# One PV run per eight units throughout, with one score unit in eight copied out of PSUM by VectorE

## The chip, the cores and the metric

One NeuronCore of a Trainium2 chip runs the whole program. The metric is the device time of one execution in microseconds. The engines are TensorE (PE; its weight loads are shown apart as PEld), VectorE (DVE), ScalarE (ACT), GpSimd (POOL) and SyncE (SP, which issues most DMAs).

## The reference

A gated sum of full attention (32 heads of 16, sequence 2048, width 512) and a SwiGLU block (inner width 1792), in float32:

```python
g = sigmoid((x * gate_w).sum(-1, keepdims=True))
q, k, v = split_heads(x @ wqkv)                    # H = 32, Dh = 16, S = 2048
a = concat_heads(softmax(q @ k.T * Dh ** -0.5) @ v) @ wo
b = (silu(x @ w1) * (x @ w3)) @ w2                 # D = 512, F = 1792
return g * a + (1 - g) * b
```

## The kernel before

A prologue (to 82 us) transposes x, splits it into a high and a low part (products of float32 accuracy are made from three products of such halves), projects v and the first heads' q and k, and bounds the scores. A tail of some 32 us ends the output projection. Between them lies the main phase, of which this case speaks. It has two streams of work that TensorE runs interleaved:

- *Attention*, in 1024 units. A unit is a pair of heads j, a half of the queries, one of 16 key blocks k and a group gq of 512 queries. `score` (L746) makes its scores: two matmuls (one per head, 50 rows each, side by side in the two row halves of the array) into a PSUM tile S of 128x1024, of which there are two (`psum2`), used in turn. ScalarE's exponential (L756) reads S and writes one of eight SBUF tiles p0 to p7 (NP = 8, list `free`). `pv` (L735) takes two units at a time: their p times V, accumulated over the key blocks in the one bank acc (17 columns for each head and query group, four column strips of the array at once). After the last key block `evac` copies acc to SBUF (L721) and stores it.
- *Products* (`feed`, L686): the remaining q/k projections, then gate and up of SwiGLU (L413), then its down projection (L531) and part of the output projection (L617). A call issues up to two matmuls, one in each row half of the array ("lanes"). A block of such matmuls fills a bank f (three banks): the first half of its sum in one lane, the second in the other, with a tiny VectorE write (tick, L713) between them that carries the order. The second half may start six slots after the first has ended, and a bank is taken again nine slots after its last use. VectorE evacuates the banks (L424 in the q/k stage, L436 and L458 in the gate and up stage, L547 and L550 later). For each gate block ScalarE makes an exponential (L441), and VectorE a scalar step (L442), eight reciprocals of 64 columns (L444) and a product (L462); these small steps are handed out one or two per unit. The ScalarE exponential of a gate block is put behind the score ahead of a PV run.

The order is written out as a string: Q is a score unit, F a call of `feed`, P a `pv` of two units. Each engine runs its instructions in the order of the program, and waits for the others only by semaphores. A PV product (P) is eight fp32 matmuls of 512 columns in two passes; a run of P's is a stretch of them without a Q or F between them. In before the string is made of 78 long periods (8 Q, 21 F, one run of 4 P) and 50 short ones (8 Q, 15 F, two runs of 2 P):

```python
one = "QQFFFFFF" + "QFFF" * 5 + "QPPPP"
two = "QFFF" * 5 + "QPPQQPP"
order = one * LONG + "QQFFF" + two * (SHORT - 1) + "QFFF" * 4 + "QPPQPP"
```

Of the kernel before, what the change touches and what calls it, by code (L numbers as in the profile page):

```python
# [11 lines left out]
AF = mybir.ActivationFunctionType  # L12
# [5 lines left out]
P = 128  # L18
S = 2048
D = 512  # L20
F = 1792
# [6 lines left out]
NPAIR = H // 2  # L28
SCALE = DH ** -0.5
# [4 lines left out]
def gated_mix_kernel(ctx: ExitStack, tc: tile.TileContext, x, wqkv, wo, w1, w3, w2, gate_w, out):  # L34
# [18 lines left out]
    nc = tc.nc  # L53
# [15 lines left out]
    QD = [[dram.tile([D, S], F32, name=f"{n}{p}_d") for p in "HL"] for n in "qk"]  # L69
# [16 lines left out]
    def psum2():  # L86
        return psum.tile([P, 2, 512], F32, name="S", bufs=2)

    def bank():
        return psum.tile([P, 512], F32, name="f", bufs=3)  # L90
# [179 lines left out]
    def load_step(s):  # L270
        half, j = divmod(s, NPAIR)
        load_q(j, half, s % 2)
        load_k(j, s % 2)
        load_guard(j, half, s % 2)
# [35 lines left out]
    splits, issued = [], 0  # L310
# [275 lines left out]
    def divide(k, half):  # L586

        yield from reciprocals(k, half)
        for b in (2 * half, 2 * half + 1):
            for _ in range(5):  # L590
                yield
            if half == 0:
                o, r = slot("hx", F32), slot("gw", F32)
            else:
                both = wk.tile([P, 2, 512], F32, name="od")
                o, r = both[:, 0, :], both[:, 1, :]
            fetch_o(k, b, o, r)
            for _ in range(7):
                yield
            nc.gpsimd.tensor_mul(o, o, r)  # L600
            for _ in range(3):
                yield
            nc.sync.dma_start(N_d[P * k:P * k + P, 512 * b:512 * b + 512], o)
            yield
        if (k, half) == (2, 1):
            load_wo(2)
# [68 lines left out]
    def after(ins, earlier):  # L675
        tc.add_manual_dep(ins.ins, earlier.ins.name,
                          mybir.DependencyInfo(mybir.DependencyClass.Sync, mybir.DependencyReason.DATA),
                          reason="the two halves of the array write a bank in turn")

    def pick(lane, rest, gap):  # L680
        if ready[lane] and (ready[lane][0]["since"] + gap <= clock or gap == 0):
            return ready[lane].pop(0)
        used = len(over) - 3
        if lane <= 1 and (used < 0 or over[used] is not None and over[used] + rest <= clock):
            block = next(source, None)
            if block:  # L686
                over.append(None)
                return dict(block=block, ps=bank(), id=len(over) - 1, n=0, turn=None)
        return None

    def feed(rest=REST, gap=GAP):
        did = 0
        for lane in range(2):
            if lanes[lane] is None:
                lanes[lane] = pick(lane, rest, gap)
        for lane in range(2):
            t = lanes[lane]
            if t is None:
                continue
            product, done, length = t["block"]  # L700
            did += 1
            second = t["turn"] is not None
            ins = product(t["ps"], slice(64 * lane, 64 * lane + 64), t["n"], second)
            if second and t["n"] == 0:
                after(ins, t["turn"])
            t["n"] += 1
            if t["n"] == length:
                lanes[lane] = None
                if second:
                    done(t["ps"])  # L710
                    over[t["id"]] = clock
                else:
                    turn = nc.vector.memset(tick[:, 0:1], 0.0)  # L713
                    after(turn, ins)
                    t.update(n=0, turn=turn, since=clock)
                    ready[1 - lane].append(t)
        return did
# [18 lines left out]
    def pv(two):  # L736
        for j, half, k, gq, n, p in two:
            for h in range(2):
                r = 32 * (2 * gq + h)
                nc.tensor.matmul(acc[r:r + DH + 1, :], V[:, k, 2 * j + h, :], p[:, h, :],  # L740
                                 start=k == 0, stop=k == NT - 1)
            free.append(n)
        if k == NT - 1:
            evac(j, half)

    def score(j, half, k, gq):  # L746
        i = (NPAIR * half + j) % 2
        ps = psum2()
        t = 512 * gq
        for h in range(2):  # L750
            r = 64 * h
            nc.tensor.matmul(ps[:, h, :], Kt[i][r:r + 50, P * k:P * k + P],  # L752
                             Qt[i][r:r + 50, t:t + 512], start=True, stop=True)
        n = free.pop(0)
        p = wk.tile([P, 2, 512], F32, name=f"p{n}")
        nc.scalar.activation(p, ps, AF.Exp, scale=SCALE)  # L756
        return j, half, k, gq, n, p


# [1 line left out]


    NP = 8
    LONG, SHORT = 78, 50
    one = "QQFFFFFF" + "QFFF" * 5 + "QPPPP"
    two = "QFFF" * 5 + "QPPQQPP"
    order = one * LONG + "QQFFF" + two * (SHORT - 1) + "QFFF" * 4 + "QPPQPP"
    free = list(range(NP))

    units = iter([(j, half, k, gq) for half in range(2) for j in range(NPAIR) for k in range(NT) for gq in range(2)])  # L770
    pend, clock = [], 0
    for i, c in enumerate(order):
        clock += 1 if c != "P" else 4
        if c == "Q":
            step = issued // 32 + 1
            if issued % 32 == 6 and step < 2 * NPAIR:
                assert 8 * (ND - 1) - qk_left >= 8 * min(step // 4, ND - 1)
                load_step(step)
            pend.append(score(*next(units)))
            issued += 1  # L780
            while splits and splits[0][0] <= issued:
                splits.pop(0)[1]()
            while soon and order[i + 1] == "P":
                soon.pop(0)()
            if issued % 128 == (40 if issued // 128 == 5 else 12) and 1 <= issued // 128 < 8:
                stages.append(divide((issued // 128 - 1) % 4, (issued // 128 - 1) // 4))
            if small or later and hurry:
                for _ in range(3 if hurry else 1 + (len(small) > (6 if len(over) < 8 * len(chunks) - 16 else 0))):
                    if small or later and hurry:
                        (small or later).pop(0)()  # L790
            if loads and (hurry or issued % 2 or len(over) > 8 * len(chunks) - 12):
                loads.pop(0)()
            for stage in stages[:1]:
                if next(stage, stages) is stages:
                    stages.pop(0)
        elif c == "F":
            feed()
        else:
            pv(pend[:2])
            pend = pend[2:]  # L800
    assert not pend and issued == 64 * NPAIR

    assert lanes[0] is None
    for _ in reciprocals(ND - 1, 1):
# [1 line left out]
    k = ND - 1  # L806
# [8 lines left out]
    for t in (NT // 2 - 2, NT // 2 - 1):  # L815
        ps = bank()
# [62 lines left out]
```

## Time and profile before

| | |
|---|---|
| time, median of 3 runs | 1406.22 us (1405.67 to 1407.54) |
| the profiled execution | 1405.92 us, span 1404.1 us |
| TensorE busy | 1397.0 us (99%) |
| ScalarE busy | 1033.6 us (74%) |
| VectorE busy | 483.6 us (34%) |
| GpSimd busy | 319.3 us (23%) |
| granted TensorE clock | full in all slices |

Times in the profile are counted from the start of the span. Matmuls are pipelined, so a busy TensorE is one that always has a matmul in flight; its pace is read from the distances between starts. A row of the timeline gives start, duration, engine, line, operation, tiles, shapes and count, and in brackets how long the engine had been idle and what ended that.

### The profile page before, as it was taken

How to read it: one execution, taken by the hardware profiler on the slowest of the kernel's cores; microseconds unless marked ns; L12 is line 12 of the kernel's file. 1: busy time of each engine (PE TensorE's matmuls, PEld its weight loads, DVE VectorE, ACT ScalarE, POOL GpSimd, SP SyncE). 2: the span in 40 equal slices, each digit the busy share in tenths (PEclk: the TensorE clock that was granted, in tenths of full speed). 3: DMA queues.
4: the chain of work that ended last, by engine and by line, in shares of the span. 5: the costliest groups of instructions: out<-in, count | busy, mean ns of one | idle time of the engine just before them, and what ended most of it. 6: DMA issues, size and time to landing. Idle time of an engine off the chain costs nothing.

```text
span 1404.1 us, 28806 instructions
## 1 busy us (share of the span) xinstructions
PE 1397.0 (99%) x11399; PEld 821.9 (59%) x11399; DVE 483.6 (34%) x1067; ACT 1033.6 (74%) x1153; POOL 319.3 (23%) x356
## 2 busy tenths in 40 slices
PE   9999999999999999999999999999999999999998
PEld 7866556566566566565565565555545555555556
DVE  4511111564555546555454654511110110110113
ACT  4557777777777777777777777788788878877880
POOL 5113433011011101110110117331323332232240
PEclk9999999999999999999999999999999999999999
DMA  7653564343123423223333336443434443354435
GB/s 205 165 123 98 132 141 113 70 116 77 46 56 85 114 54 80 66 67 96 70 77 68 82 78 170 106 96 82 126 84 97 106 108 69 70 128 108 104 120 178
DMA packets 112670, 141.43 MB, mean 101 GB/s; under 512 B 16400, under 2 KB 70672, under 8 KB 109456
## 3 DMA queue, kind: packets, MB, share of 16 engines
q1 hardware_dynamic: 110384, 135.72, 40.1%
q10 hardware_dynamic: 2144, 3.80, 0.8%
q8 instruction: 92, 1.51, 0.5%
q14 instruction: 50, 0.41, 0.1%
HBM read 90.70 MB, written 48.76 MB: 99 GB/s over the span
## 4 chain that ended last, share of the span: by engine, by line
PE 99%; DVE 0%; ACT 0%; issue 0%; ACTq 0%
PE acc L740 33%; PE f L413 27%; PE S L752 20%; PE f L531 11%; PE S L184 2%; PE f L96 1%; PE f L98 1%; PE f L97 1%; PE f L617 1%; PE acc L338 0%; PE S L97 0%; PE S L96 0%; PE S L98 0%; PE f L158 0%; PE S L158 0%; ACT xH L161 0%
## 5 line engine op out<-in xcount | busy, mean ns | idle before, releaser
L756 ACT ACTIVATE p<-S 128x1024 f32<-128x1024 f32 x1024 | 967.8, 1027 | 300.8 <-PE S L752 300.8
L740 PE MATMUL acc<-p,V 128*17 128x512 f32 x4096 | 474.4, 594 | 0.0
L752 PE MATMUL S<-Qt,Kt 50*128 50x512 f32 x2048 | 403.7, 408 | 1.0 <-DVE V L396 0.7
L752 PEld LDWEIGHTS S<-Qt,Kt 50*128 50x128 f32 x2048 | 183.3, 184 | 185.5 <-ACT p L756 84.9
L740 PEld LDWEIGHTS acc<-p,V 128*17 128x17 f32 x4096 | 102.3, 97 | 272.5 <-issue 272.3
L444 DVE RECIPROCAL sg<-sg 128x64 f32<-128x64 f32 x448 | 209.3, 517 | 49.1 <-issue 47.0
L413 PE MATMUL f<-xH,fl 64*128 64x512 f32 x1088 | 217.5, 392 | 0.0
L413 PE MATMUL f<-xL,fh 64*128 64x512 f32 x1088 | 217.4, 390 | 0.0
L413 PE MATMUL f<-xH,fh 64*128 64x512 f32 x1088 | 217.4, 392 | 0.0
L413 PEld LDWEIGHTS f<-xH,fh 64*128 64x128 f32 x1088 | 104.4, 186 | 23.8
L413 PEld LDWEIGHTS f<-xL,fh 64*128 64x128 f32 x1088 | 104.3, 185 | 23.4
L413 PEld LDWEIGHTS f<-xH,fl 64*128 64x128 f32 x1088 | 104.6, 186 | 22.6 <-POOL fl L314 0.3
L713 DVE MEMSET tick<- 1x1 f32 x190 | 11.2, 59 | 274.5 <-PE f L531 156.1
L313 POOL CAST fh<-fr 128x512 fp32r<-128x512 f32 x34 | 21.6, 636 | 355.7 <-DMA fr<-in_B_w_dram 292.2
L436 DVE COPY gs<-f 128x512 f32<-128x512 f32 x56 | 38.7, 691 | 69.7 <-PE f L413 63.4
L531 PE MATMUL f<-xL,fh 64*128 64x512 f32 x208 | 61.8, 390 | 0.0
L531 PE MATMUL f<-xH,fl 64*128 64x512 f32 x208 | 60.8, 390 | 0.0
L531 PE MATMUL f<-xH,fh 64*128 64x512 f32 x208 | 59.8, 390 | 0.0
L531 PE MATMUL f<-xH,raw 64*128 64x512 f32 x192 | 57.3, 390 | 0.0
L442 DVE TENSOR_SCALAR sg<-sg 128x512 f32<-128x512 f32 x56 | 27.7, 494 | 82.9 <-ACT sg L441 77.6
L600 POOL TENSOR_TENSOR hx<-hx,gw 128x512 f32<-128x512 f32 x8 | 10.3, 1287 | 198.7 <-DMA gw<-r_d 188.2
L721 DVE COPY u<-acc 128x512 f32<-128x512 f32 x32 | 22.1, 692 | 94.7 <-PE acc L740 91.5
(216 smaller groups left out, 1277.0 us busy)
## 6 DMA issues: line engine op xcount, KB each, us to landing
Kt<-kH_d SPq DMA_DIRECT2D x128, 128.0 KB
h_d<-sg SPq DMA_DIRECT2D x56, 256.0 KB
sg<-h_d SPq DMA_DIRECT2D x43, 256.0 KB
fr<-in_B_w_dram SPq DMA_DIRECT2D x42, 256.0 KB
Qt<-qH_d SPq DMA_DIRECT2D x128, 64.0 KB
Kt<-kL_d SPq DMA_DIRECT2D x64, 128.0 KB
Qt<-qL_d SPq DMA_DIRECT2D x64, 64.0 KB
b_d<-y SPq DMA_DIRECT2D x16, 256.0 KB
```

The costliest lines, as they stand in the source:

```text
L96: nc.tensor.matmul(ps, sH, mH, start=first, stop=False)
L184: nc.tensor.matmul(ps[:, i, :], w[i][h][:, k, :], xs[b][:, k, :], start=n == k == 0, stop=n == 2 and k == ND - 1)
L313: nc.gpsimd.tensor_copy(hi, src)
L413: return nc.tensor.matmul(ps, w[i == 1][r, k, :], (xL if i == 2 else xH)[b][r, k, :], start=n == 0 and not second, stop=n == 3 * ND - 1 an ...
L436: nc.vector.tensor_copy(gs, ps)
L442: small.append(lambda: nc.vector.tensor_scalar(sg, sg, 1.0, None, op0=OP.add))
L444: small.append(lambda q=q: nc.vector.reciprocal(sg[:, q:q + 64], sg[:, q:q + 64]))
L531: ins = nc.tensor.matmul(ps, hs[t][q][i == 1][r, P * o:P * o + P], (w2L if i == 2 else w2H)[q][r, o, :], start=n == 0 and not second, stop ...
L721: nc.vector.tensor_copy(u, acc)
L740: nc.tensor.matmul(acc[r:r + DH + 1, :], V[:, k, 2 * j + h, :], p[:, h, :], start=k == 0, stop=k == NT - 1)
L752: nc.tensor.matmul(ps[:, h, :], Kt[i][r:r + 50, P * k:P * k + P], Qt[i][r:r + 50, t:t + 512], start=True, stop=True)
L756: nc.scalar.activation(p, ps, AF.Exp, scale=SCALE)
```

## The change

The order is built from two new periods, 128 in all. Each has 8 units and one run of four P; `wide` has 19 F, `tight` 18, and the total of F's stays 2388 (so 84 wide periods come first, then 44 tight ones). In each period the fifth unit is written D: its scores are copied from S to its SBUF tile p by VectorE (L757 of after), and its exponential is formed in place, p to p, at the letter e (L805), which stands behind the sixth unit. The other seven units keep their exponential from PSUM (L756 before, L760 after). The tile p of a D unit is handed to `pv` as before.

```diff
-    def score(j, half, k, gq):
+    def score(j, half, k, gq, wait):
...
         p = wk.tile([P, 2, 512], F32, name=f"p{n}")
-        nc.scalar.activation(p, ps, AF.Exp, scale=SCALE)
+        if wait:
+            nc.vector.tensor_copy(p, ps)
+            raw.append(p)
+        else:
+            nc.scalar.activation(p, ps, AF.Exp, scale=SCALE)
...
-    LONG, SHORT = 78, 50
...
+    PERIODS, PRODUCTS = 128, 2388
+    tight = "QFFQFFFFQFFQFFFDFFFQeFFFFQQPPPP"
+    wide = "QFFQFFFFQFFFQFFDFFFQFFeFFFQQPPPP"
+    n_wide = PRODUCTS - PERIODS * tight.count("F")
+    order = wide * n_wide + tight * (PERIODS - n_wide)
...
-        clock += 1 if c != "P" else 4
-        if c == "Q":
+        clock += {"P": 4, "e": 0}.get(c, 1)
+        if c in "QD":
...
-            pend.append(score(*next(units)))
+            pend.append(score(*next(units), c == "D"))
...
+        elif c == "e":
+            p = raw.pop(0)
+            nc.scalar.activation(p, p, AF.Exp, scale=SCALE)
```

TensorE before, in the stretch of short periods: two PV runs of eight matmul pairs (rows acc<-p,V) with two score units (S<-Qt,Kt, x4) between them:

```order
L752 MATMUL S<-Qt_109,Kt_112 128x512 x2
L740 MATMUL acc<-p_18340,V 17x512 x2
L740 MATMUL acc<-p_18345,V 17x512 x2
L740 MATMUL acc<-p_18358,V 17x512 x2
L740 MATMUL acc<-p_18369,V 17x512 x2
L752 MATMUL S<-Qt_108,Kt_111 128x512 x4
L740 MATMUL acc<-p_18380,V 17x512 x2
L740 MATMUL acc<-p_18398,V 17x512 x2
L740 MATMUL acc<-p_18409,V 17x512 x2
L740 MATMUL acc<-p_18428,V 17x512 x2
L752 MATMUL S<-Qt_108,Kt_111 128x512 x2
```

TensorE in the changed kernel, at the end of one of its tight periods: two score units, then the whole run:

```order
L752 MATMUL S<-Qt_108,Kt_111 128x512 x4
L740 MATMUL acc<-p_18680,V 17x512 x2
L740 MATMUL acc<-p_18689,V 17x512 x2
L740 MATMUL acc<-p_18704,V 17x512 x2
L740 MATMUL acc<-p_18713,V 17x512 x2
L740 MATMUL acc<-p_18725,V 17x512 x2
L740 MATMUL acc<-p_18736,V 17x512 x2
L740 MATMUL acc<-p_18757,V 17x512 x2
L740 MATMUL acc<-p_18762,V 17x512 x2
L752 MATMUL S<-Qt_109,Kt_112 128x512 x2
```

The two scores that stood between the two half runs now stand ahead of one whole run, so a run of all eight units follows at once. ScalarE in the changed kernel, one period in the gate and up stage (p0 to p7 are the SBUF tiles of its units, S the PSUM tile):

```order
L760 ACTIVATE p0_11932<-S_11929 128x1024
L760 ACTIVATE p1_11943<-S_11940 128x1024
L760 ACTIVATE p2_11960<-S_11957 128x1024
L760 ACTIVATE p3_11972<-S_11969 128x1024
L760 ACTIVATE p5_11998<-S_11995 128x1024
L805 ACTIVATE p4_11985<-p4_11985 128x1024
L760 ACTIVATE p6_12026<-S_12023 128x1024
L760 ACTIVATE p7_12033<-S_12030 128x1024
L441 ACTIVATE sg_11981<-gs_11979 128x512
```

The exponential of the fifth unit (p4) has moved behind that of the sixth (p5), and reads p4 itself; before, ScalarE formed all eight from S in the order of the units. VectorE, another period of the same stage in the changed kernel, around one of the new copies (L757):

```order
L442 TENSOR_SCALAR sg<-sg 128x512
L444 RECIPROCAL sg<-sg 128x64 x5
L713 MEMSET tick 1x1
L444 RECIPROCAL sg<-sg 128x64 x3
L462 TENSOR_TENSOR sg<-raw,sg 128x512
L757 COPY p_13436<-S 128x1024
L442 TENSOR_SCALAR sg<-sg 128x512
L444 RECIPROCAL sg<-sg 128x64
```

The copy stands in the middle of VectorE's work for the gate blocks, which before had its queue to itself and the evacuations.

More of the change, by code (lines that the diff above doesn't have):

```diff
@@ L755, in score @@
         p = wk.tile([P, 2, 512], F32, name=f"p{n}")
-        nc.scalar.activation(p, ps, AF.Exp, scale=SCALE)
+        if wait:
[3 more added lines that the diff above has]
+            nc.scalar.activation(p, ps, AF.Exp, scale=SCALE)
         return j, half, k, gq, n, p
     NP = 8
-    LONG, SHORT = 78, 50
-    one = "QQFFFFFF" + "QFFF" * 5 + "QPPPP"
-    two = "QFFF" * 5 + "QPPQQPP"
-    order = one * LONG + "QQFFF" + two * (SHORT - 1) + "QFFF" * 4 + "QPPQPP"
+    PERIODS, PRODUCTS = 128, 2388
[3 more added lines that the diff above has]
+    order = wide * n_wide + tight * (PERIODS - n_wide)
     free = list(range(NP))
     units = iter([(j, half, k, gq) for half in range(2) for j in range(NPAIR) for k in range(NT) for gq in range(2)])
-    pend, clock = [], 0
+    pend, raw, clock = [], [], 0
     for i, c in enumerate(order):
-        clock += 1 if c != "P" else 4
-        if c == "Q":
+        clock += {"P": 4, "e": 0}.get(c, 1)
+        if c in "QD":
             step = issued // 32 + 1
@@ L800, in gated_mix_kernel @@
             pend = pend[2:]
-    assert not pend and issued == 64 * NPAIR
+    assert not pend and not raw and issued == 64 * NPAIR
     assert lanes[0] is None
```

## The prediction

> **What bounds the kernel now.** I read the page first: busy times, the chain that ended last, the costliest groups.
>
> ```profile
> PE 1397.0 (99%) x11399; PEld 821.9 (59%) x11399; DVE 483.6 (34%) x1067; ACT 1033.6 (74%) x1153; POOL 319.3 (23%) x356
> PE 99%; DVE 0%; ACT 0%; issue 0%; ACTq 0%
> L756 ACT ACTIVATE p<-S 128x1024 f32<-128x1024 f32 x1024 | 967.8, 1027 | 300.8 <-PE S L752 300.8
> ```
>
> TensorE is the bound: it is never idle, the chain lies on it, and ScalarE's 300.8 us of idle time before the exponentials all ended at a score. So a change pays only if it shortens TensorE's own stream, and costs whatever it makes TensorE wait. The timeline shows what that stream is made of. First a period of the long kind (eight units, one PV run), then one of the short kind (eight units, two runs):
>
> ```profile
> 602.84 0.39 PE L752 MATMUL S<-Qt,Kt 50*128 50x512 f32 x2
> 603.16 3.63 PE L740 MATMUL acc<-p,V 128*17 128x512 f32 x32
> 606.72 0.50 PE L752 MATMUL S<-Qt,Kt 50*128 50x512 f32 x2
> ...
> 607.32 7.54 ACT L756 ACTIVATE p<-S 128x1024 f32<-128x1024 f32 x8 [1.93 <-PE S L752]
> ...
> 613.34 0.39 PE L752 MATMUL S<-Qt,Kt 50*128 50x512 f32 x2
> 613.66 3.63 PE L740 MATMUL acc<-p,V 128*17 128x512 f32 x32
> 617.22 0.50 PE L752 MATMUL S<-Qt,Kt 50*128 50x512 f32 x2
> ```
>
> ```profile
> 1105.17 1.91 PE L740 MATMUL acc<-p,V 128*17 128x512 f32 x16
> 1107.01 0.74 PE L752 MATMUL S<-Qt,Kt 50*128 50x512 f32 x4
> 1107.68 1.91 PE L740 MATMUL acc<-p,V 128*17 128x512 f32 x16
> 1109.52 0.50 PE L752 MATMUL S<-Qt,Kt 50*128 50x512 f32 x2
> 1110.55 0.40 PE L752 MATMUL S<-Qt,Kt 50*128 50x512 f32 x2
> 1111.48 0.39 PE L752 MATMUL S<-Qt,Kt 50*128 50x512 f32 x2
> ...
> 1114.58 1.91 PE L740 MATMUL acc<-p,V 128*17 128x512 f32 x16
> ```
>
> A long period takes 617.22 - 606.72 = 10.50 us, a short one 1114.58 - 1105.17 = 9.41 us. A slot (one score unit or one pair of products) takes 0.232 us: four of them lie between 1110.55 and 1111.48. The four after a PV run take 1.03 (1109.52 to 1110.55). From the last score to its PV run it is 0.32 (613.34 to 613.66), from the start of a four-product run to the next score 3.56 (603.16 to 606.72).
>
> The change will bring scores closer to the exponentials that free their buffers, so the price of that hand-off is needed. Before shows it once, where the long periods end and a third score comes only five slots after the first. The chain of waits there has ScalarE in it:
>
> ```profile
> 901.25 1.03 ACT L756 ACTIVATE p<-S 128x1024 f32<-128x1024 f32 x1 [2.44 <-PE S L752]
> 902.32 0.18 PEld L752 LDWEIGHTS S<-Qt,Kt 50*128 50x128 f32 x2 [0.68 <-ACT p L756]
> 902.32 0.51 PE L752 MATMUL S<-Qt,Kt 50*128 50x512 f32 x2 [0.26 <-ACT p L756]
> 902.66 0.40 PE L531 MATMUL f<-xL,raw 64*128 64x512 f32 x1
> ```
>
> The exponential ends at 902.28, the score's weight load starts 0.04 to 0.05 later, and the score runs 0.51 instead of 0.39 to 0.40: its weights were not loaded ahead, which costs 0.11. So a score takes effect 1.03 + 0.05 + 0.11 = **1.19 us after the start of the exponential that frees its buffer**, never sooner.
>
> **The change, part by part.**
>
> *50 PV runs fewer.* Products (2388), units (1024) and PV products (512) stay; the runs go from 178 to 128. If TensorE never waited, the period of 18 products would take 9.78: score 2 comes at 0.80 (1.03 less a slot), score 8 is 22 slots later at 5.90, then 0.32 and 3.56. The period of 19 has a slot more: 10.02. 84 x 10.02 + 44 x 9.78 = 1272.0. Before, the same work runs from the first score to the end of the last PV run:
>
> ```profile
> 81.96 0.47 PE L752 MATMUL S<-Qt,Kt 50*128 50x512 f32 x1 [0.72 <-DVE V L396]
> ...
> 1370.11 2.29 PE L740 MATMUL acc<-p,V 128*17 128x512 f32 x16
> ```
>
> That is 1372.40 - 81.96 = 1290.4 us. So by TensorE alone the change saves 18.4 us (0.37 per run).
>
> *New spacing of the scores.* There are two S buffers, so a score waits for the exponential (or copy) of the unit two before it. I walk one period from its first score (0), with the 1.19, with exponentials that follow each other at 0.92 and start 0.49 after a score (0.60 after the first, whose weights come late). The 0.60 is 606.72 to 607.32; the 0.49 is 613.34 to the last of the eight, which started at 607.32 + 7.54 - 1.03 = 613.83; the 0.92 is (7.45 - 1.03)/7 from the first eight, where ScalarE was kept fed:
>
> ```profile
> 82.82 7.45 ACT L756 ACTIVATE p<-S 128x1024 f32<-128x1024 f32 x8 [9.10 <-PE S L752]
> ```
>
> Exponentials 1 to 4 start at 0.60, 1.52, 2.43, 3.35 in both kinds. Period of 18: score 3 at 1.96 (may from 1.79). Score 4 at 2.65, but may only from 1.52 + 1.19 = 2.71. Score 5 (the copied one) at 3.64 (may from 3.62), score 6 at 4.57 (may from 4.54), its exponential at 5.06. Score 7 at 5.73. Score 8 is due at 5.96, six slots after score 6, and may from 5.06 + 1.19 = 6.25: **a wait of 0.29**, with the whole PV run queued behind it. PV at 6.57, next period at **10.13** instead of 9.78. Period of 19: score 5 is due at 3.59 and may from 3.62, score 6 at 4.55, its exponential at 5.04, score 8 due at 6.17 and may from 6.23; next period at **10.11** instead of 10.02. Both kinds come out at the same length because the same chain sets it: four exponentials, score 6, its exponential, score 8. Waits: 84 x 0.09 + 44 x 0.35 = 23.0 us. Sum of the two parts: 84 x 10.11 + 44 x 10.13 = 1294.9, and 0.1 from the last run's end, so **4.6 us more** than before. A row read 0.05 off in this chain moves it by 128 x 0.05 = 6.4 us.
>
> *The exponential in place from SBUF.* It stands behind exponential 6 on ScalarE, starts about 5.97 and is out of the chain. Units 5 to 8 are needed by the third and fourth PV products, the last at about 6.57 + 2.6; exponential 8 ends at 5.06 + 3 x 0.92 + 1.03 = 8.85. It hides, with 0.3 to spare; if that cover were gone each 0.1 would cost 12.8 us.
>
> *The copy on VectorE.* No such copy is in the trace; the nearest row is a 128x1024 pass out of the same S tile, and the weight load that waited for it:
>
> ```profile
> 9.21 1.23 DVE L162 TENSOR_TENSOR xL<-S,xH 128x1024 fp32r<-128x1024 f32 x1
> 10.48 0.19 PEld L184 LDWEIGHTS S<-xL,wh 128*128 128x128 f32 x1 [0.50 <-DVE xL L162]
> ```
>
> So 1.23, the same 0.04 to 0.05 after it, and score 7 may from 3.64 + 0.49 + 1.23 + 0.05 + 0.11 = 5.52: 0.21 early in the period of 18, 0.44 in that of 19, and the wait of score 8 behind it hides 0.29 and 0.06 more. So the copy may start **0.5 us late** for nothing. VectorE takes its queue in order, so what stands ahead of the copy decides:
>
> ```profile
> 604.25 1.14 ACT L441 ACTIVATE sg<-gs 128x512 f32<-128x512 f32 x2
> 604.91 0.43 DVE L442 TENSOR_SCALAR sg<-sg 128x512 f32<-128x512 f32 x1 [1.17 <-ACT sg L441]
> 605.37 1.38 DVE L444 RECIPROCAL sg<-sg 128x64 f32<-128x64 f32 x3
> ...
> 235.00:907.00 672.00, 671.74 (x5762) 397.90 (x5760) 359.09 (x804) 511.45 (x570) 95.73 (x98) 1.00 0.35 81
> L436 DVE COPY gs<-f 128x512 f32<-128x512 f32 x56 | 38.7, 691 | 69.7 <-PE f L413 63.4
> L721 DVE COPY u<-acc 128x512 f32<-128x512 f32 x32 | 22.1, 692 | 94.7 <-PE acc L740 91.5
> ```
>
> In the gate stage (235 to 907 before) VectorE is busy 53% of the time, and its work for a gate block starts only when that block's exponential (L441) ends, now behind exponential 8: about 8.85 + 0.5 = 9.35. The next copy is due at 10.11 + 3.62 + 0.49 = 14.2. That leaves 4.9 us, 5.4 with the spare. By the order of the program between 3.3 and 6.2 us stand there (a scalar step 0.43, six to nine reciprocals at 0.46 to 0.52, one or two evacuations at 0.69, sometimes L721), and 8 of some 65 periods have more than 5.4: over by 3 to 8 us in all. Bounds: 0 (work done earlier) and about 20 (one more 0.69 in each of the 41 periods that begin so, less what is spare). I take 4.
>
> In the q/k stage before that, VectorE sometimes stands at the head of its queue for a buffer:
>
> ```profile
>   issue: 13.2, 5
>   DMA kL_d<-gs: 8.9, 2
>   DMA qL_d<-gs: 4.8, 2
> ```
>
> These waits (for L424, up to 6 us, 9 of 24) held nobody; now a copy can stand behind one, and TensorE behind the copy. They are 26.9 of the 153 us from the first score to 235, so 18% of 15 copies are hit, at some 0.5 us beyond the spare: I take 1, at most 10. Small ticks and bank evacuations behind the copy have six to nine slots and mostly a PV run to spare: nothing, at most 3.
>
> **Sum**, against the profiled execution: 1405.9 + 4.6 + 5 = **1415.5 us**. The median of the three runs is 0.3 above that execution, well below my error, so I give the same number for it.
>
> **The rivals.**
>
> *Faster: the hand-off is shorter than I read it.* If no score waited, only the run ends would count: 1405.9 - 18.4 = 1387.5. If just the weights of a waiting score were loaded ahead, the hand-off would be 1.19 - 0.11 = 1.08, the period of 18 would take 9.96 (score 8 from 5.00 + 1.08) and that of 19 its 10.02, in all 1279.9: 1395.4 us. Against both speaks the row at 902.32: the weight load itself started only after the exponential. Chance together 0.16. The Trainium skill has a rule for the second version ("TensorE: Matmul & The Clock Gate", Part 3, The mechanism): TensorE pulls a weight load ahead of matmuls in flight. The trace agrees for loads that wait for nothing (they start a slot ahead of their matmul), and disagrees for this one.
>
> *Slower by much: VectorE's queue decides.* If the copy of a gate-stage period is late by an evacuation and a reciprocal beyond what I counted (0.69 + 0.52 - 0.5 = 0.7 us, for a third of 65 periods), 15 us come on top: 1431. It decides from the point at which a copy starts 0.5 us late. For it: 53% busy with a queue in order; against it: in before VectorE idles 1.17 us ahead of L442 and longer ahead of the evacuations, so it catches up. Chance 0.14.
>
> *No change:* the walk is 0.03 us per period too long and the copy never late: 1402 to 1409. Chance 0.15.
>
> That the change doesn't do what it says is excluded by the order of the program: 128 runs of sixteen PV matmuls, 128 copies.
>
> **How the numbers follow.** My forecast, the walk with some lateness of the copies (1409 to 1425), has 0.55, the three rivals 0.45. A measurement of this kernel tells about 0.2% (2.8 us) from no change. Faster by more: the first rival and 0.03 of the third, 0.19; within: the rest of the third and the low end of the forecast, 0.14; slower: the rest of the forecast and the second rival, 0.67. The range takes in the second version of the first rival and the second rival up to about its price, 1395 to 1430; what is left out is no score waiting at all, and copies later still.
>
> **What would show it.** In the profile of the changed kernel: PV runs 10.1 us apart in both stretches of the order, not 10.0 and 9.8; TensorE idle before L752, put down to exponentials (about 0.3 a period in the last third); VectorE's copy at 1.2 us; few waits of L752 for VectorE, and those in the gate stage. Periods of 10.0 and 9.8 would prove the hand-off wrong; waits for VectorE beyond 10 us would make the second rival right.

## The result, and the profile after

| | before | after |
|---|---|---|
| median | 1406.56 us (1405.67 to 1407.54) | 1426.56 us (1425.14 to 1426.76) |
| profiled execution, span | 1404.1 us | 1424.5 us |
| VectorE busy | 483.6 us (34%) | 627.2 us (44%) |

The changed kernel takes 1.014 times as long, interval 1.0122 to 1.0157: 20 us slower. Forecast were 9.3 us more (1415.5), with the range up to 1430. The sign and the range held, and the size was less than half of what came.

The page after, busy times, the chain, and the groups of exponentials, copies and exponentials in place:

```profile
PE 1411.9 (99%) x11399; PEld 821.4 (58%) x11399; DVE 627.2 (44%) x1195; ACT 1040.3 (73%) x1153; POOL 318.9 (22%) x356
PE 94%; DVE 3%; ACT 1%; issue 1%; DMA 0%; SPq 0%; DVEq 0%; ACTq 0%
L760 ACT ACTIVATE p<-S 128x1024 f32<-128x1024 f32 x896 | 866.1, 1024 | 310.7 <-PE S L752 308.4
L757 DVE COPY p<-S 128x1024 f32<-128x1024 f32 x128 | 156.5, 1223 | 81.3 <-PE S L752 76.5
L805 ACT ACTIVATE p<-p 128x1024 f32<-128x1024 f32 x128 | 134.2, 1049 | 1.0 <-DVE p L757 0.5
```

TensorE is "busy" 14.9 us longer though it has the same number of matmuls: a stalled one counts as in flight, so the sign that the prediction named, TensorE idle before scores for exponentials, is 0.4 us in its own rows. VectorE is new on the chain with 3%. The waits of TensorE's weight loads (engine, tile, line, what it waited for, us in total, times, longest) are more telling:

```profile
PEld S L752 <- ACT p L760: 86.8, 377, 0.7
PEld f L413 <- DVE tick L713: 8.0, 9, 2.7
PEld S L752 <- DVE tick L713: 0.9, 2, 0.6
PEld S L752 <- DVE p L757: 0.8, 3, 0.4
```

Scores wait for exponentials 377 times, about three in each of the 128 periods. The row of before was:

```profile
PEld S L752 <- ACT p L756: 84.9, 100, 0.9
```

The totals of the two rows are nearly equal, but they are not alike. Those of before are two scores in each short period that stand behind a PV run, where the weight loads lie idle for 0.85 us anyway. So the number of waits tells more here than their sum. For the new copy scores wait five times, 1.7 us in all: the two waits of scores that the view puts down to a tick are such waits too, since by the program no score depends on a tick, and both loads start 0.05 us after a copy has ended (906.35 and 949.22). Products wait for ticks, which had no row in before. One of the first 84 periods (19 products) in the timeline:

```profile
164.09 0.50 PE L752 MATMUL S<-Qt,Kt 50*128 50x512 f32 x2
...
164.72 3.80 ACT L760 ACTIVATE p<-S 128x1024 f32<-128x1024 f32 x4 [1.90 <-PE S L752]
...
168.26 1.23 DVE L757 COPY p<-S 128x1024 f32<-128x1024 f32 x1 [0.51 <-PE S L752]
168.57 0.19 PEld L752 LDWEIGHTS S<-Qt,Kt 50*128 50x128 f32 x2 [0.17 <-ACT p L760]
...
169.18 1.03 ACT L760 ACTIVATE p<-S 128x1024 f32<-128x1024 f32 x1 [0.65 <-PE S L752]
...
170.10 1.05 ACT L805 ACTIVATE p<-p 128x1024 f32<-128x1024 f32 x1
170.25 0.19 PEld L752 LDWEIGHTS S<-Qt,Kt 50*128 50x128 f32 x2 [0.22 <-ACT p L760]
...
170.68 3.63 PE L740 MATMUL acc<-p,V 128*17 128x512 f32 x32
...
174.24 0.51 PE L752 MATMUL S<-Qt,Kt 50*128 50x512 f32 x2
```

This is the walked chain: four exponentials (164.72 on), score 6 (its weight load at 168.57 waited for the fourth), its exponential (169.18 to 170.21), score 8 (weight load at 170.25, 0.04 after that end), the PV run. From first score to first score it is 174.24 - 164.09 = 10.15. The exponential in place (170.10) is out of the chain. Two PV runs of the last 44 periods, which hold one product less, are as far apart (1112.56 - 1102.41):

```profile
1102.41 3.63 PE L740 MATMUL acc<-p,V 128*17 128x512 f32 x32
...
1112.56 3.63 PE L740 MATMUL acc<-p,V 128*17 128x512 f32 x32
```

Most of the 127 distances between PV runs are 10.13 to 10.19. Sixteen are longer, by 0.14 to 2.47, fifteen of them before 930 us; together they are 8.7 us over 10.15. In eleven of them a product waits for a tick (7.3 us), in one a score waits for a late copy (0.4). The other four (1.1 us) have neither: there a score waits 0.36 to 0.48 us for an exponential where it is otherwise about 0.2, and why is not shown. Here is how one of the eleven (PV runs at 527.66 and 538.80, 11.14 apart) came about:

```profile
535.69 1.22 DVE L757 COPY p<-S 128x1024 f32<-128x1024 f32 x1
536.82 0.42 DVE L442 TENSOR_SCALAR sg<-sg 128x512 f32<-128x512 f32 x1
537.28 1.03 DVE L444 RECIPROCAL sg<-sg 128x64 f32<-128x64 f32 x2
537.77 0.06 DVE L713 MEMSET tick<- 1x1 f32 x1
...
537.91 0.19 PEld L413 LDWEIGHTS f<-xH,fh 64*128 64x128 f32 x2 [1.19 <-DVE tick L713]
```

No one waited for the copy. But the tick stands behind the copy, a scalar step and a reciprocal, and the second half of a block of products waited 1.19 us for it, with every later score and PV run in TensorE's queue behind.

At the end the last PV run is followed by eight products of the output projection, before the tail's own begin (L96):

```profile
1387.12 3.63 PE L740 MATMUL acc<-p,V 128*17 128x512 f32 x32
1390.68 0.50 PE L617 MATMUL f<-xH,fl 64*128 64x512 f32 x1
...
1392.74 0.51 PE L96 MATMUL f<-xH,raw 128*128 128x512 f32 x1
```

Before has none there: its last PV run ends at 1372.40, 31.7 us before the span's end; here it is 33.75.

### The profile page after: what moved, and what is told of

Read it like the earlier page. It is cut to its first block, busy times and chain, and to the rows that moved or that the text cites. A ratio compares the mean times of both kernels' runs of the same rounds, so it can differ in the third digit from the quotient of the medians.

```text
span 1424.5 us, 28902 instructions
## 1 busy us (share of the span) xinstructions
PE 1411.9 (99%) x11399; PEld 821.4 (58%) x11399; DVE 627.2 (44%) x1195; ACT 1040.3 (73%) x1153; POOL 318.9 (22%) x356
## 4 chain that ended last, share of the span: by engine, by line
PE 94%; DVE 3%; ACT 1%; issue 1%; DMA 0%; SPq 0%; DVEq 0%; ACTq 0%
PE acc L740 30%; PE f L413 25%; PE S L752 19%; PE f L531 11%; PE S L184 1%; DVE sg L444 1%; PE f L96 1%; PE f L98 1%; PE f L97 1%; PE f L617 1%; ACT p L760 1%; DVE p L757 1%; DVE sg L442 0%; DMA Kt<-kH_d 0%; PE acc L338 0%
## 5 line engine op out<-in xcount | busy, mean ns | idle before, releaser
L760 ACT ACTIVATE p<-S 128x1024 f32<-128x1024 f32 x896 | 866.1, 1024 | 310.7 <-PE S L752 308.4
L752 PE MATMUL S<-Qt,Kt 50*128 50x512 f32 x2048 | 426.5, 422 | 2.1 <-DVE V L396 0.8
L413 PE MATMUL f<-xH,fh 64*128 64x512 f32 x1088 | 269.4, 394 | 4.3 <-DVE tick L713 4.3
L413 PE MATMUL f<-xL,fh 64*128 64x512 f32 x1088 | 268.3, 392 | 0.0
L413 PE MATMUL f<-xH,fl 64*128 64x512 f32 x1088 | 268.3, 391 | 0.0
L444 DVE RECIPROCAL sg<-sg 128x64 f32<-128x64 f32 x448 | 209.1, 519 | 8.6 <-issue 6.4
L757 DVE COPY p<-S 128x1024 f32<-128x1024 f32 x128 | 156.5, 1223 | 81.3 <-PE S L752 76.5
L413 PEld LDWEIGHTS f<-xH,fh 64*128 64x128 f32 x1088 | 138.0, 186 | 27.5 <-DVE tick L713 8.0
L413 PEld LDWEIGHTS f<-xH,fl 64*128 64x128 f32 x1088 | 138.2, 186 | 19.5
L413 PEld LDWEIGHTS f<-xL,fh 64*128 64x128 f32 x1088 | 138.1, 186 | 19.0
L805 ACT ACTIVATE p<-p 128x1024 f32<-128x1024 f32 x128 | 134.2, 1049 | 1.0 <-DVE p L757 0.5
L531 PE MATMUL f<-xH,fl 64*128 64x512 f32 x208 | 62.3, 392 | 0.0
L531 PE MATMUL f<-xL,fh 64*128 64x512 f32 x208 | 61.9, 393 | 0.0
L531 PE MATMUL f<-xH,fh 64*128 64x512 f32 x208 | 60.0, 392 | 0.0
```

The costliest lines, as they stand in the source:

```text
L413: return nc.tensor.matmul(ps, w[i == 1][r, k, :], (xL if i == 2 else xH)[b][r, k, :], start=n == 0 and not second, stop=n == 3 * ND - 1 an ...
L444: small.append(lambda q=q: nc.vector.reciprocal(sg[:, q:q + 64], sg[:, q:q + 64]))
L531: ins = nc.tensor.matmul(ps, hs[t][q][i == 1][r, P * o:P * o + P], (w2L if i == 2 else w2H)[q][r, o, :], start=n == 0 and not second, stop ...
L757: nc.vector.tensor_copy(p, ps)
L805: nc.scalar.activation(p, p, AF.Exp, scale=SCALE)
```

## The experiments

Theory A: the period's length is set by the hand-off chain, whatever the number of products. Theory B: the copy and what is queued around it on VectorE cost most. Theory C: TensorE's own stream is longer than walked. Times are medians; ratios are to the kernel before.

**Shorter exponentials.**

```diff
...
-V[:, k, 2 * j + h, :], p[:, h, :],
+V[:, k, 2 * j + h, :], p[:, h:h + 1, 0:256].to_broadcast([P, 2, 256]),
...
-nc.scalar.activation(p, ps, AF.Exp, scale=SCALE)
+nc.scalar.activation(p[:, :, 0:256], ps[:, :, 0:256], AF.Exp, scale=SCALE)
```

(and the same for the exponential in place)

> The changed kernel with half of the exponential left out: ScalarE forms only the first 256 of each 512 columns of p, and PV reads those columns twice, so that TensorE's work and VectorE's copy are as in the changed kernel. Theory A (the length of a period is set by the hand-off from exponential to score): no score waits any more, the PV runs come 10.03 us apart in the first 84 periods and 9.80 in the last 44, not 10.15; 127 spacings give 26 us less, with the late periods of the gate stage kept, a span of about 1398 us. Theory B (late periods, ticks and copies on VectorE's queue, are most of the loss): a span of 1415 or more, and spacings of 10.15. Theory C (TensorE's own work is longer than I walked it): no change, 1424.

Measured: 1400.3 us, ratio 0.9959 (0.9944 to 0.9973), span 1398.5. Exponential from PSUM in its groups, two PV runs of the first stretch and two of the last:

```profile
L760 ACT ACTIVATE p<-S 128x512 f32<-128x512 f32 x896 | 522.0, 598 | 662.4 <-PE S L752 640.2
```

```profile
300.52 3.63 PE L740 MATMUL acc<-p,V 128*17 128x512 f32 x32
310.54 3.63 PE L740 MATMUL acc<-p,V 128*17 128x512 f32 x32
...
1106.58 3.63 PE L740 MATMUL acc<-p,V 128*17 128x512 f32 x32
1116.38 3.63 PE L740 MATMUL acc<-p,V 128*17 128x512 f32 x32
```

10.02 and 9.80: the natural lengths of the walk, to 0.02. So C is out, and the waits for exponentials are worth 26 us of span. The late periods stayed (7.8 us in all). With them, this order would beat before by only 6 us even if no score had to wait for an exponential any more.

**No copy.**

```diff
-tight = "QFFQFFFFQFFQFFFDFFFQeFFFFQQPPPP"
-wide = "QFFQFFFFQFFFQFFDFFFQFFeFFFQQPPPP"
+tight = "QFFQFFFFQFFQFFFQFFFQFFFFQQPPPP"
+wide = "QFFQFFFFQFFFQFFQFFFQFFFFFQQPPPP"
```

> The changed kernel with the copied unit made an ordinary one (D becomes Q, e goes): all eight exponentials from PSUM, one PV run per eight units. Theory A (hand-off chain): six exponentials now stand in the chain, the period becomes 10.32 in both stretches instead of 10.15, 22 us more, less the late periods of the gate stage of 8.8 us: a span of about 1437 us. Theory B (the copy and what is queued behind it on VectorE cost most of the loss): faster than the changed kernel, 1416 or less.

Measured: 1437.68 us, ratio 1.0223 (1.0206 to 1.024), span 1435.9; the period 10.28 to 10.30 in both stretches, late periods only 2.1 us. So theory B is out in this order: without its copy the kernel is slower. The copy does what it is for, 0.14 us a period by taking one exponential out of the chain (127 x 0.14 = 18 us), and it pays 6.6 us of late periods for it. One run per eight units without it costs 31 us.

**The copy alone, in the old order** (the lines against the kernel before; the rest of its order stays).

```diff
-one = "QQFFFFFF" + "QFFF" * 5 + "QPPPP"
-two = "QFFF" * 5 + "QPPQQPP"
+one = "QQFFFFFF" + "QFFF" * 2 + "DFFFQFeFFQFFF" + "QPPPP"
+two = "QFFF" * 2 + "DFFFQFeFFQFFF" + "QPPQQPP"
```

> The kernel before with the same copy and exponential in place for one unit in eight, its PV runs and its two kinds of period kept. Theory A with a small price for the copy: its periods keep 10.50 and 9.41, and only the lateness behind VectorE's queue is added: 2 to 9 us, a span of 1406 to 1413. Theory B (the copy is most of the loss): 15 to 20 us more than before, 1419 to 1424.

Measured: 1427.41 us, ratio 1.0147 (1.013 to 1.0164), span 1425.7. That is a little above theory B's number (1419 to 1424), and my expectation missed. Scores now do wait for the copy:

```profile
PEld S L752 <- DVE p L757: 21.4, 72, 1.4
PEld S L752 <- DVE tick L713: 6.6, 21, 1.5
```

(The second row is again waits for copies: each of the 21 loads starts 0.05 us after a copy has ended.)

One of these, VectorE and TensorE:

```profile
428.12 0.69 DVE L458 TENSOR_TENSOR raw<-f,gs 128x512 f32<-128x512 f32 x1 [1.16 <-PE f L413]
...
428.73 1.21 DVE L757 COPY p<-S 128x1024 f32<-128x1024 f32 x1
...
430.00 0.19 PEld L752 LDWEIGHTS S<-Qt,Kt 50*128 50x128 f32 x2 [0.49 <-DVE p L757]
```

The old order puts the score that needs the buffer eight slots (1.85 us) behind the copied one; 0.49 + 1.23 + 0.05 + 0.11 = 1.88 is already over that, and here an evacuation of 0.69 stood ahead. In the changed order the same score has time to spare, so there the copy itself holds a score only five times. The price of the copy is thus one of its place. Neither part of the change is cheap alone (+21 for the copy, +31 for the runs), and both together cost +20.

**The short periods alone with one run.** The 50 short periods of before keep their 15 products (the line against the kernel before; the long periods have no copy):

```diff
-two = "QFFF" * 5 + "QPPQQPP"
+two = "QFFQFFFQFFFQFDFQFFeFQFFQPPPP"
```

> The kernel before with its 50 short periods alone changed: 15 calls of feed as before, but one PV run of four products instead of two of two, and one copied unit (QFFQFFFQFFFQFDFQFFeFQFFQPPPP). The long periods have no copy. Theory A (hand-off chain): a period with one run takes 10.16 us whether it holds 15, 18 or 19 products, so these 50 go from 9.41 to 10.16: 37 us more, a span of about 1441. If TensorE's own work sets the length: 9.11, 15 us less, 1389.

Measured: 1444.94 us, ratio 1.0271 (1.0254 to 1.0288), span 1443.1.

```profile
1099.72 3.63 PE L740 MATMUL acc<-p,V 128*17 128x512 f32 x32
1109.82 3.63 PE L740 MATMUL acc<-p,V 128*17 128x512 f32 x32
```

10.10 with 15 products, as 10.15 with 18 or 19: three or four products of 0.232 are worth nothing there. With the two lengths of the run with shorter exponentials, theory A is shown. The old short period, cut by two runs, took 9.41.

**The late periods.** Four runs change what can make a tick late. First, no reciprocals (L444):

```diff
-small.append(lambda q=q: nc.vector.reciprocal(sg[:, q:q + 64], sg[:, q:q + 64]))
+pass
```

> The changed kernel with the eight reciprocals of each gate block (L444) left out, which is 210 of VectorE's 627 us; everything else stays. Theory A with late periods from VectorE's queue: the 16 late periods of the gate stage (8.7 us in all) go, the spacing stays at 10.15: a span of about 1416 us. Rival (the late periods come from the tight order itself, or from ScalarE's steps of the gate blocks): they stay, 1424.

Measured: 1420.42 us, ratio 1.0104 (1.0088 to 1.0119), span 1418.5. Late periods are down from 8.7 to 1.1 us, the four without a tick; the spacing stays at 10.15; the tail is 1 us longer. Next, the small steps held back at the copied unit:

```diff
-if small or later and hurry:
+if (small or later and hurry) and (c != "D" or hurry):
```

> The changed kernel with the small steps of the gate blocks (scalar step, reciprocals, product) held back at the copied unit, so that none is put right behind the copy there; they go to the other seven units. If the late periods come from ticks that stand behind the copy and the small steps together: part of their 8.7 us goes, a main phase 3 to 6 us shorter, a span of 1418 to 1421. If the copy alone makes the ticks late, or the steps only move behind the next ticks: no change, 1423 to 1424.

Measured: 1422.57 us, ratio 1.0115 (1.0098 to 1.0132), span 1420.9; late periods 4.2 us. The wait for ticks falls from 8.0 to

```profile
PEld f L413 <- DVE tick L713: 1.6, 4, 0.8
```

Only one of its late periods (0.8 us) is left to a tick; the others have late copies or waits for exponentials. In the run without copies one period, too, is late by a tick (0.9 us). So of 7.3 us 0.8 is left without the steps behind the copy, 0.9 without the copy, and nothing without the reciprocals: neither the copy nor the reciprocals alone make the ticks late by much, but the one behind the other does. Then a later second half:

```diff
-REST, GAP = 9, 6
+REST, GAP = 9, 8
```

> The changed kernel with the second half of a block of products allowed two positions of the order later after the first has ended (GAP 8, not 6), so that a tick may be some 0.5 us later for nothing; the queues are otherwise as in the changed kernel. If the late periods come from ticks that stand behind the copy and the reciprocals: about half of their 8.7 us goes, a span of 1419 to 1421. If they come from late copies: no change, 1424.

Measured: 1425.16 us, ratio 1.0139 (1.0123 to 1.0154), span 1423.5, late periods 8.1 us. A miss: some of the small ones halved, the large ones stayed. In the period shown above TensorE again waited 1.2 us for its tick, so this constant does not set the distance there. Last, ticks on another engine:

```diff
-turn = nc.vector.memset(tick[:, 0:1], 0.0)
+turn = nc.gpsimd.memset(tick[:, 0:1], 0.0)
```

> The changed kernel with the ticks (L713) written by GpSimd instead of VectorE, nothing else moved. If the late periods come from ticks that stand behind the copy or the reciprocals on VectorE: 6 to 8 of the 8.7 us go, a span of 1416 to 1419. If they come from late copies or late bank evacuations: no change, 1424. If a tick on GpSimd is itself late (it stands behind that engine's passes): some late periods more, above 1424.

Measured: 1470.02 us, ratio 1.0448 (1.0432 to 1.0464). The third case came: ticks wait behind GpSimd's own work, and behind the DMAs that this work waits for (before the tick at 931.02 GpSimd idled 7.04 us for a DMA, then made its passes).

```profile
PE f L413 <- POOL tick L713: 24.5, 7, 8.3
PE f L531 <- POOL tick L713: 7.6, 3, 3.9
```

It says nothing on the copy, but shows how directly a late tick becomes TensorE's time.

**Twelve more calls of feed.**

```diff
-PERIODS, PRODUCTS = 128, 2388
+PERIODS, PRODUCTS = 128, 2400
```

> The changed kernel with 12 more calls of feed in the order (96 wide periods, not 84), so that the eight slots of products that were left for after the last PV run go into the main phase. Theory A (18 or 19 products make no difference to a period's length): spacings stay at 10.15, the 2 us between the last PV run and the tail go, a span of about 1422.5. If TensorE's own work set the length of a period, the 12 wide periods would be 0.23 us longer each and nothing would be gained: 1424 to 1425.

Measured: span 1421.6; the tail's first matmul (L96) now follows the last PV run at once, and the twelve more wide periods are 10.15 like the rest:

```profile
1386.31 3.63 PE L740 MATMUL acc<-p,V 128*17 128x512 f32 x32
1389.87 0.50 PE L96 MATMUL f<-xH,raw 128*128 128x512 f32 x1
```

From the end of the PV run to the span's end it is 31.7 again. The median is 1425.16 us (1423.47 to 1427.6), which overlaps the changed kernel's, so the 2 us are shown by the trace, not by the times.

**A search for something better.** First, three copies in each of 40 periods at the end, the rest as before:

```diff
...
+LONG, SHORT, THREE = 58, 30, 40
...
+mixed = "DQFFeFFFFDQFFFFeFFDQFFFFFeFQQPPPP"
+order = one * LONG + "QQFFF" + two * (SHORT - 1) + "QFFF" * 4 + "QPPQPP" + mixed * THREE
```

> Copies where VectorE is lightly used, with the kernel before as its base: 58 long and 30 short periods as in before, then, in the last 400 us, 40 periods of 18 products and one PV run with three copied units each (DQFFeFFFFDQFFFFeFFDQFFFFFeFQQPPPP). The chain of exponentials in the walk is shortened by copies in it: by the walk 9.91 us, where a long and a short period take 19.91 together. Theory A: 40 x 9.91 instead of 20 x 19.91 is 2 us less than before, 4 if the walk is again 0.05 too long: a span of 1400 to 1402. If a copy costs time wherever it stands: 1408 or more.

Measured: 1405.97 us, ratio 0.9998 (0.9989 to 1.0007), span 1403.4: no difference. Most of the new periods are 9.89 to 9.95, as walked:

```profile
1109.12 3.63 PE L740 MATMUL acc<-p,V 128*17 128x512 f32 x32
1119.01 3.20 PE L740 MATMUL acc<-p,V 128*17 128x512 f32 x28
```

The last PV run ends 1.6 us sooner than in before, and 0.9 of it goes to products left for the tail. Then a unit split between the engines, so that S should come free after 0.7 us. The first run has three such units in every period, the second only in its last 57 periods (of 17 products), behind 71 periods of 20 products without a copy. The lines that form a split unit are the same:

```diff
 if wait:
-    nc.vector.tensor_copy(p, ps)
-    raw.append(p)
+    nc.scalar.activation(p[:, 0, :], ps[:, 0, :], AF.Exp, scale=SCALE)
+    nc.vector.tensor_copy(p[:, 1, :], ps[:, 1, :])
+    raw.append(p[:, 1, :])
```

> The changed kernel with its copied unit replaced by three split ones in each period (84 periods of 19 products, then 44 of 18): of a split unit ScalarE forms the exponential of one head from PSUM while VectorE copies the other head's 512 columns, whose exponential is formed in place later. Its S buffer comes free after 0.7 us instead of 1.03 or 1.23. Theory A: with this in the chain no score waits, the periods are 10.03 and 9.80 us, the PV runs saved pay, and with late periods of the gate stage as in the changed kernel (8 us) the span is about 1398. If the three copies of a period stand late on VectorE's queue in the gate stage, each period there is 0.1 to 0.2 us longer: 1406 to 1415.

> As the last, but with the copies only where VectorE is lightly used: first 71 periods of 20 products and one PV run without any copy, then 57 periods of 17 products with three split units each. Theory A: the first kind waits hardly (10.29, as without the copy), the second comes to its natural 9.57 to 9.66; 71 x 10.29 + 57 x 9.6 = 1278 us where before has 1290.4, with 2 to 4 us of late periods a span of 1394 to 1396. If the split unit's two halves free the buffer no sooner than a whole exponential, the second kind takes 10.1: a span of 1420.

Measured: 1508.7 us (ratio 1.0729, 1.0715 to 1.0744) and 1478.28 us (1.0506, 1.0491 to 1.052). Split units of the second:

```profile
1104.66 0.60 ACT L757 ACTIVATE p<-S 128x512 f32<-128x512 f32 x1 [2.15 <-PE S L752]
...
1105.30 0.69 DVE L758 COPY p<-S 128x512 f32<-128x512 f32 x1 [4.61 <-ACT p L757]
1106.04 0.19 PEld L752 LDWEIGHTS S<-Qt,Kt 50*128 50x128 f32 x2 [0.74 <-DVE p L758]
```

The two halves run one behind the other: the copy waits for ScalarE's half. S comes free 1.33 us after the half exponential starts (1105.99 - 1104.66), later than with a whole one (1.03), and most of the periods of 17 products took 10.8 to 10.9, more than the 10.1 that the expectation gave for that case. So these runs tried a longer hand-off, not a shorter one. What a split with both halves at the same time would give was not tried.

## Why the prediction was right or wrong

Its steps against the changed kernel's own span (20.4 us more; forecast 9.6):

- *50 runs fewer save 18.4 us*: right as the natural length, shown where no score waits (10.02 and 9.80).
- *The hand-off of 1.19, and one length for both kinds*: right. Walked 10.11 and 10.13, measured 10.15. The Trainium skill's rule of weight loads that are pulled ahead ("TensorE: Matmul & The Clock Gate", Part 3, The mechanism) again does not reach a load that waits for its buffer: the one at 170.25 starts only after the exponential.
- *Sum of the walk, +4.6*: mis-sized, the largest share of the miss. From first score to last PV end it is 18.2 us more, less 8.7 of late periods: 9.5. The period is 0.04 (19 products) or 0.02 (18) longer than walked (84 x 0.04 + 43 x 0.02 = 4.2): the first exponential starts 0.63 after its score (164.09 to 164.72), not 0.60. The first period cost another 0.6 (82.13 to 89.26, walked 6.57). The prediction priced this: 0.05 in the chain is 6.4 us.
- *Lateness, +5*: mis-sized, and for another reason than given. It was 8.7 us, but only 0.4 of it from a late copy (scores wait 1.7 us for copies in all), where the prediction took 5. The step that failed is "Small ticks and bank evacuations behind the copy have six to nine slots and mostly a PV run to spare: nothing, at most 3": late ticks cost 7.3 us. The copy was followed as an instruction that may be late, and too little as one that makes those behind it late.
- *The tail, nothing*: it cost 2.0 us. That the new order leaves eight products over could have been seen in the order of TensorE's last rows.
- *The exponential in place is hidden*: right.

4.9 + 3.7 + 2.0 = 10.6 us of the miss of 10.8; the rest is the first score, 0.2 later than in before (82.13 against 81.96). So the chain that sets the period was foreseen, and the size came out at less than half by two things: rows read a few hundredths too short, times 128, and ticks and tail put at nothing (of the 5 us for late copies 0.4 came). The faster rival (a shorter hand-off) fell with the weight load at 170.25. The slower rival (VectorE's queue decides through late copies) had the right engine and, in this order, the wrong victim. In the old order the run with the copy alone is just what that rival describes.

## What to carry to other kernels

With two buffers between a producer and a consumer, count the hand-offs in a period before taking other work out of it: below that floor (10.1 us here, with one unit copied) less work of the producer saves nothing, and only a shorter or rarer hand-off does. When an instruction is added to an in-order queue, price it twice: what it waits for at its place, and who waits for each small instruction behind it, down to a 0.06 us tick. The same copy saved 11 us in one order (1426.56 against 1437.68 without it) and cost 21 in another (1427.41 against 1406.55), so measure an operation where it will stand.

## What the runs showed of the hardware

An exponential of 128x512 from PSUM takes 0.598 us, one of 128x1024 1.024, and one of 128x1024 in place in SBUF 1.049, no less than from PSUM. VectorE's copy of 128x1024 out of PSUM takes 1.223, as the nearest row of before (1.23) had it.
